# Forgetting attention and a SwiGLU block in one kernel: batch 0's queries and keys loaded and turned by two heads instead of four, and the gates of its first query tiles by one-hot matmuls

## The chip, the cores and the metric

One core of a Trainium2 chip runs the whole kernel. The metric is the device time of a run in microseconds. Its five engines have a queue each: PE (matmuls), DVE (vector), ACT (scalar functions), POOL (GpSimd: masks, casts and the issue of some DMAs) and SP (issue of the other DMAs).

## The reference

Batch 8, 8 heads, 576 positions, head size 64; then 4608 tokens of 512 features through a feed-forward block of 1536.

```python
def _attn_ref(q, k, v, f):
    scores = scale * np.matmul(q, k.transpose(0, 1, 3, 2))
    log_f = np.log(np.clip(f, 0.0001, 1.0))
    cum = np.cumsum(log_f, axis=-1)
    decay = cum[:, :, :, None] - cum[:, :, None, :]
    scores = np.where(causal, -1000000000.0, scores + decay)
    attn = np.exp(scores - np.max(scores, axis=-1, keepdims=True))
    attn = attn / (np.sum(attn, axis=-1, keepdims=True) + 1e-09)
    return np.matmul(attn, v)

def _moe_ref(x, w_gate, w_val, w_out):
    g = x @ w_gate
    return (g / (1.0 + np.exp(-g)) * (x @ w_val)) @ w_out
```

The attention output, with heads side by side, is `x` of the second function.

## The kernel before

The work is recorded as operations, each with an engine, a cost, what it comes after, buffers that it takes, and a key. `Plan.run` goes through time with these costs, and gives each engine the ready operation with the lowest key whose buffers are free. So the order on every engine is fixed when the kernel is built, by costs, keys and `ready` times; on the chip each engine works its queue in that order and waits on semaphores. PSUM has eight banks in four pools: `f` (4), `s` (2), `o` (1), `t` (1).

Attention of one head has scores in transposed form (keys on partitions, queries along the free axis), cut into the four `BANKS` so that nothing above the causal diagonal's blocks is computed. Bank 0 holds the first 256 queries (two tiles of 128). For each bank: scores on PE, `expo` on ACT (with the scale), `mask` on POOL for the diagonal blocks, `weigh` on PE against V with a column of ones, which gives the sum for the division. `invert` and `scale` on DVE divide, `flip` on PE turns the result, `put` copies it into `xT`, which the feed-forward part (`gate`, `tanh`, `silu`, `times`, `project`) reads.

The decay is added inside the score matmuls. For batches 1 to 7 four more rows of queries and keys carry it (a high, middle and low part of the key's cumulated logarithm, and the query's), brought through DRAM by `dec_out` and `rows`.

Batch 0 can't wait for that. Its gates are laid out in `KG` and `QG`, 128 partitions each, four groups of 32 rows: `KG` has the high part of the keys in rows 0 to 31 (`hi` for `hi0`), ones in rows 32 to 63, middle and low parts in rows 64 to 127 (`mid`, `low`); `QG` has ones, and the query's cumulated value in rows 32 to 63 (`up`). `choose` multiplies `QG` by a column of `chosen`, which is one in the four rows of one head and zero elsewhere: `G0[h]` for the first 256 queries and `G1[h]` for the rest. A matmul of `KG` with such a tile adds the decay of that head. The chain that makes them is recorded in `gates`: loads of `f`, `clip` (DVE), `ln` (ACT), `scan` (DVE), then `up` and `hi0` (ACT), `hi`, `rest1`, `mid`, `low` (DVE), for the first 256 columns and then for the other 320. The same for batch 1 to 7 (`lf1`) is begun in the same place.

Batch 0's queries and keys come in by `ld_quad`, each with 128 partitions: two neighbouring heads (64 partitions each) and, along the free axis, the two heads four further. `turn` transposes them on PE in two steps of 5 and 4 blocks into two banks, and `straighten` copies the bank to `QK`. The pair of heads `jj` and `jj + 4` is then scored together by `score2` on the two halves of the array, followed by the gate matmuls. While the kernel starts, and nothing is ready, `dummy` gives PE a matmul of the identity on 256 columns.

The constants (`blank`) are filled by DVE at the start: the ones in `KG` and `QG` ("lay"), in V's columns, in `PT` ("pt") and in `ones`. `warm` loads ACT's tables. `PACE0` sets from which planned time on the loads of batch 2 and later may go.

Of the kernel before, what the change touches and what calls it, by code (L numbers as in the profile page):

```python
# [33 lines left out]
class Plan:  # L34
# [150 lines left out]

HALF = 256
BANKS = [
    [(0, 0, 256), (1, 128, 128)],
# [11 lines left out]
PACE_A = 8.8  # L200
PACE0 = 64.0
LEAD = 14.0
# [3 lines left out]
def kernel(ctx, tc, q, k, v, f, w_gate, w_val, w_out, out):  # L206
# [44 lines left out]
    OT = [sb(f"ot{i}", [P, DM], F32) for i in range(NOT)]  # L251
    ident = sb("ident", [P, P], BF16)
    chosen = sb("chosen", [P, H], F32)
    warm = sb("warm", [1, 1], F32)
# [12 lines left out]
    REST = S - HALF  # L267
    G0 = [xT[:, 3, 2 * S + HALF * n : 2 * S + HALF * (n + 1)] for n in range(4)]
    G0 += [xT[:, r, S + HALF * n : S + HALF * (n + 1)] for r in (2, 3) for n in range(2)]
    G1 = [xT[:, n // 3, 2 * S + REST * (n % 3) : 2 * S + REST * (n % 3 + 1)] for n in range(H)]  # L270
# [51 lines left out]
    def clip(e, lf, c):  # L322
        nc.vector.tensor_scalar(out=lf[:, c], in0=lf[:, c], scalar1=1e-4, scalar2=1.0, op0=ALU.max, op1=ALU.min)

# [45 lines left out]

    def choose(e, h, part):
        c = slice(0, HALF) if part == 0 else slice(HALF, S)
        nc.vector.tensor_scalar_mul((G1 if part else G0)[h], QG[:, c], chosen[:, h : h + 1])  # L373

    def gates(parts, key):
# [3 lines left out]
        done, s = [], None  # L379
        a = op(("DVE", 0.45), clip, lf, slice(0, S), after=lds, key=key)  # L380
        lns = [op(("ACT", 0.15 + (c.stop - c.start) / 1100), ln, lf, c, after=[a], key=key + 0.1 * i, tag="ln")
               for i, c in enumerate(parts)]
        for i, c in enumerate(parts):
            kk = key + 11 * i
            w = c.stop - c.start
            s = op(("DVE", 0.1 + w * 0.0024), scan, cum, lf, c, after=[lns[i], s], key=kk, tag="scan")
            u = op(("ACT", 0.15 + w / 1100), up, c, after=[s, o_lay], key=kk + 0.1, tag="up")
            h = op(("DVE", 0.05 + w * 0.0011), hi, slice(64, P), c, after=[s], key=kk, tag="hi")
            h0 = op({"ACT": 0.15 + w / 1100, "DVE": 0.05 + w * 0.0011}, hi, slice(0, GR), c, after=[s, o_lay], key=kk + 0.2, tag="hi0")
            r = op(("DVE", 0.05 + w * 0.0015), rest1, c, after=[h], key=kk)  # L390
            m = op(("DVE", 0.05 + w * 0.0011), mid, c, after=[r], key=kk)
            l = op(("DVE", 0.05 + w * 0.0013), low, c, after=[m], key=kk, tag="low")
            done.append([u, h0, l])
        every = [x for d in done for x in d]
        outs = [op(("SP", SPi), dec_out, 0, n, after=every, key=-7, dma=0.15, packet=50, tag="decout") for n in range(4)]
        a = op(("DVE", 0.45), clip, lf1, slice(0, S), after=[ld1], key=key + 0.3)
        a = op(("ACT", 0.67), ln, lf1, slice(0, S), after=[a], key=key + 0.3, tag="ln1")
# [11 lines left out]
    def blank(e, what):  # L409
        if what == "qk":  # L410
            nc.vector.memset(QK[:, :, 1, 2 * S :], 0.0)
        elif what == "pt":
            for t in PT:
                for c in PADS:
                    nc.vector.memset(t[:, c : c + D], 1.0)  # L415
        elif what == "edge":
            nc.sync.dma_start(out=qk_dram[:, HSD:], in_=QK[: 2 * B, 0, 1, 2 * S :])
        elif what == "ones":
            nc.vector.memset(ones, 1.0)
        elif what == "ones_q":  # L420
            nc.sync.dma_start(out=dec_dram[0, 1], in_=ones)
        elif what == "ones_k":
            nc.sync.dma_start(out=dec_dram[1:, 0].rearrange("r h s -> h r s"),
                              in_=ones.unsqueeze(1).to_broadcast([BH, 3, S]))
        elif what == "lay":
            nc.vector.memset(QG, 1.0)
            nc.vector.memset(KG[GR : 2 * GR], 1.0)
        elif what == "chosen":
            nc.vector.tensor_add(chosen, ident[:, :H], ident[:, GR : GR + H])
            for r in (64, 96):  # L430
                nc.vector.tensor_add(chosen, chosen, ident[:, r : r + H])
        else:
            nc.vector.memset(VB[what][:, :, :, D:], 1.0)
            nc.vector.memset(VB[what][LAST:, NB - 1], 0.0)
# [3 lines left out]
              after=[op(("DVE", 0.07), lambda e: nc.vector.memset(warm, 1.0), key=-30)])  # L438
    o_lay = op(("DVE", 0.5), blank, "lay", key=-29)
    dec0, out0, out1 = gates(SPLIT, -25)  # L440
    o_warm = op(("ACT", 1.4), lambda e: nc.scalar.activation(warm, cum[:1, :1], AF.Exp), after=[dec0[0][0]], key=-19.5)
    o_id = op(("POOL", 0.6), lambda e: make_identity(nc, ident[:, :]), key=-18)
    o_vb = [op(("DVE", 0.45), blank, i, key=-7 if i < FIRST else 40 + 2000 * i, ready=0 if i < FIRST else 15) for i in range(NVB)]
    o_chosen = op(("DVE", 0.4), blank, "chosen", after=[o_id], key=-26)
    picked = [[op(("DVE", 0.33), choose, h, part, after=[o_chosen] + [d[0] for d in dec0[: part + 1]] + (dec0[0] + dec0[1] if part else []),
                  key=PICK_KEY[part][h % 4], tag=("pick", part, h)) for h in range(H)]
              for part in range(2)]
    o_qkz = op(("DVE", 0.5), blank, "qk", key=-6)
    o_pt = op(("DVE", 1.2), blank, "pt", key=-5)
    o_ones = op(("DVE", 0.3), blank, "ones", key=-6)  # L450
    o_edge = op(("SP", SPi), blank, "edge", after=[o_qkz], key=900, dma=0.2, ready=22)
# [18 lines left out]

    PH = [[(0, 5, 0), (5, 4, 0)], [(t, n, u) for u in range(2) for t, n in ((0, 5), (5, 4))]]

    def turn(e, b, g, x, n, bt):
        t0, nt, u0 = PH[b][n]
        t = ps(bt).bitcast(BF16)
        for i in range(nt):
            for u in range(2) if b == 0 else [u0]:
                r = slice(D * (u - u0), D * (u - u0 + 1))
                nc.tensor.transpose(t[r, i * P : (i + 1) * P], QN[b][2 * g + x][:, u, (t0 + i) * D : (t0 + i + 1) * D], ident)  # L479

    def straighten(e, b, g, x, n, bt):
        t0, nt, u = PH[b][n]
        slot, r = (hq2[b][g].i, slice(0, P)) if b == 0 else (hqk[b * FB + 2 * u + g].i, slice(0, D))
        dst = QK[r, slot, x, : 2 * S].rearrange("p (j c t) -> p j c t", j=2, t=QT)[:, :, :, t0 : t0 + nt]
# [60 lines left out]
    turns, rows1 = [], []  # L545

    def quad(b, g, key, ready=0.0):
        done = [[], []]
        for x in range(2):
            kk = key + x  # L550
            o1 = op(("POOL", SW), ld_quad, b, g, x, key=kk, dma=1.8, packet=107, ready=ready, tag=("quad", b, g, x))
            for n, (t0, nt, u) in enumerate(PH[b]):
                bt = Buf("t", ("f", TURN_F))
                o2 = op(("PE", (1.5 if b == 0 else 1.0) * mm(*[P] * nt)), turn, b, g, x, n, bt, after=[o1, o_id], take=[bt],
                        key=kk, tag=("turn", b, g, x))
                turns.append(o2)
                done[u].append(op(
                    {"ACT": act(nt * P), "DVE": dve(nt * P)}, straighten, b, g, x, n, bt, after=[o2, o_qkz],
                    use=[bt, hq2[b][g] if b == 0 else hqk[b * FB + 2 * u + g]], key=kk, tag=("str", b, g, x)))
        if b == 0:  # L560
            for j in range(2):
                q_ready[0, 2 * g + j] = done[0]
        else:
            for u in range(2):
                p = b * FB + 2 * u + g
                r = op(("SP", SPi), rows, p, after=[o_qkz] + out0 + o_out1, use=[hqk[p]], key=key, dma=0.25, ready=ready,
                       tag=("rows", p))
                rows1.append(r)
                for j in range(2):
                    q_ready[2 * p + j] = done[u] + [r]  # L570

# [30 lines left out]
    def score2(e, b, jj, i, bs):  # L602
# [13 lines left out]
        for n, (kt, q0, w, c) in enumerate(segs):  # L616
            for u in range(2):
                s, h, end = ps(bs[u]), jj + 4 * u, n == len(segs) - 1
                m = min(P, S - kt * P)
                g, q1 = (G0[h], q0) if i == 0 else (G1[h], q0 - HALF)  # L620
                nc.tensor.matmul(s[:m, c : c + w], KG[:, kt * P : kt * P + m], g[:, q1 : q1 + w], start=False, stop=end)  # L621

# [93 lines left out]
    def attention2(b, key, parts):  # L716

        bx = {}
        for n, (bks, qb, nq) in enumerate(parts):
            ahead = len(parts) > 1 and n == 0  # L720
            got = {}
            for jj in range(4):
# [4 lines left out]
                for m, i in enumerate(bks):  # L727
                    bs = [Buf("s", ("f", F_UNTIL)) for _ in range(2)]
                    segs = [x[2] for x in BANKS[i]]
                    cost = mm(*segs) * 3 + 0.2  # L730
                    gate_rows = dec0[i > 0] + dec0[0] + [picked[i > 0][h % H] for h in heads]
                    a = op(("PE", cost), score2, b, jj, i, bs, after=q_ready[b, jj] + gate_rows, take=bs,
# [126 lines left out]

    quad(0, 0, -20)  # L860
    quad(0, 1, -15)
    for n in range(NB):
# [35 lines left out]
V1_KEY = 400  # L898
PICK_KEY = ((-19.5, -18.5, -14.5, -14.4), (0.5, 100.5, 200.5, 300.5))
V1_AT = 16.0  # L900
# [43 lines left out]
```

## Time and profile before

| | |
|---|---|
| runs, us | 389.14, 389.13, 389.35 (median 389.14) |
| profiled execution, us | 389.19 |
| its span, us | 387.5 |
| PE busy | 377.8 us, 98% of the span, 3097 matmuls |
| DVE, ACT, POOL busy | 221.0, 214.4, 140.1 us |
| PE's clock granted | 1.0 |
| landing of batch 0's loads (queries, keys, queries, keys) | 6.35, 7.81, 9.93, 11.86 us |

Times within the execution are counted in microseconds from the start of the span; `L479` is line 479 of the kernel. In rows of groups the figures after the bar are busy us and mean ns of one, then idle time ahead of them. In the timeline they are start and duration, in brackets the idle time ahead and what ended it. Matmuls are pipelined: those in a row start sooner after each other than one lasts.

### The profile page before, as it was taken

The page shows a single profiled execution, that of the slowest core. Times are in us where ns is not written, and L with a number is a line of the kernel's source. Part 1 is how long each engine was busy: PE and PEld are TensorE (multiplying, and loading weights), DVE is VectorE, ACT ScalarE, POOL GpSimd, SP SyncE. Part 2 cuts the span into 40 slices and gives each one's busy share as a digit, 9 for nine tenths or more (in the row PEclk, how much of TensorE's full clock was granted, in tenths as well). Part 3 has the DMA queues.
Part 4 walks back from the last instruction along what each step waited for, and adds up shares of the span by engine and source line. Part 5 has one row for each costly group of instructions (what it writes and reads, how often), then busy time and mean ns, then how long its engine had stood idle before and what let it go on. Part 6 is the DMA issues. An engine that isn't in the chain of part 4 may idle for free.

```text
span 387.5 us, 8340 instructions
## 1 busy us (share of the span) xinstructions
PE 377.8 (98%) x3097; PEld 216.3 (56%) x3097; DVE 221.0 (57%) x466; ACT 214.4 (55%) x442; POOL 140.1 (36%) x368
## 2 busy tenths in 40 slices
PE   5999999999999999999999999999999999999995
PEld 3667889456556555555555555555554444444442
DVE  8958978247723774176525872376427725733750
ACT  4989974266656465755667457557673323323321
POOL 8796647036433452444355236513330000000000
PEclk9999999999999999999999999999999999999999
DMA  8999997689477998999699949994231011002002
GB/s 152 198 189 193 210 201 121 136 188 193 96 142 179 190 156 116 214 230 184 124 190 234 180 94 217 194 184 82 65 89 44 0 57 54 1 29 81 2 17 91
DMA packets 122760, 51.50 MB, mean 133 GB/s; under 512 B 109792, under 2 KB 116960, under 8 KB 121952
## 3 DMA queue, kind: packets, MB, share of 16 engines
q1 hardware_dynamic: 106336, 35.68, 45.7%
q0 software_dynamic: 16288, 15.14, 26.8%
q8 instruction: 24, 0.39, 0.4%
q14 instruction: 16, 0.13, 0.1%
q10 hardware_dynamic: 96, 0.15, 0.1%
HBM read 38.63 MB, written 17.11 MB: 144 GB/s over the span
## 4 chain that ended last, share of the span: by engine, by line
PE 94%; DVE 4%; ACT 1%; issue 0%; DVEq 0%; ACTq 0%
PE ps L793 48%; PE ps L808 24%; PE ps L596 10%; PE ps L648 7%; PE ps L479 1%; PE ps L621 1%; DVE xT L373 1%; PE ps L665 1%; PE ps L614 1%; DVE QK L304 1%; DVE PT L415 0%; DVE xT L330 0%; ACT xT L326 0%; ACT QK L302 0%; ACT QK L326 0%
## 5 line engine op out<-in xcount | busy, mean ns | idle before, releaser
L801 DVE SCALAR_TENSOR_TENSOR th<-th,ps 128x512 f32<-128x512 f32 (+1 forms) x120 | 75.6, 630 | 70.6 <-ACT th L797 70.4
L797 ACT ACTIVATE th<-ps 128x512 f32<-128x512 f32 (+1 forms) x120 | 66.5, 554 | 87.1 <-PE ps L793 85.0
L793 PE MATMUL ps<-xT,wv 128*128 128x512 bf16 (+1 forms) x480 | 113.0, 357 | 0.0
L793 PE MATMUL ps<-xT,wg 128*128 128x512 bf16 (+1 forms) x480 | 112.9, 357 | 0.0
L625 ACT ACTIVATE PT<-ps 128x320 bf16<-128x320 f32 (+2 forms) x192 | 92.2, 507 | 24.9 <-PE ps L596 17.0
L808 PE MATMUL ps<-wo,hh 128*128 128x512 bf16 x432 | 104.4, 379 | 0.0
L804 DVE TENSOR_TENSOR hh<-th,ps 128x512 bf16<-128x512 f32 (+1 forms) x120 | 76.1, 634 | 12.9 <-PE ps L793 1.2
L634 POOL TENSOR_SCALAR_AFFINE_SELECT PT<-PT 128x128 bf16<-128x128 bf16 (+1 forms) x192 | 52.6, 279 | 74.2 <-ACT PT L625 69.0
L793 PEld LDWEIGHTS <-wg 128*128 128x128 bf16 x480 | 45.2, 97 | 39.1
L793 PEld LDWEIGHTS <-wv 128*128 128x128 bf16 x480 | 45.5, 97 | 36.7
L596 PE MATMUL ps<-QK 68*128 68x256 bf16 x392 | 64.2, 261 | 0.0
L808 PEld LDWEIGHTS <-hh 128*128 128x128 bf16 x432 | 40.9, 97 | 38.8
L634 POOL TENSOR_SCALAR_AFFINE_SELECT PTa<-PTa 128x256 bf16<-128x256 bf16 x64 | 25.9, 408 | 74.3 <-ACT PTa L625 72.7
L655 DVE RECIPROCAL rc<-ps 128x5 f32<-128x5 f32 (+2 forms) x68 | 12.9, 190 | 62.1 <-PE ps L648 61.9
L648 PEld LDWEIGHTS <-PT 128*128 128x128 bf16 x768 | 36.8, 97 | 13.6
L648 PE MATMUL ps<-VB,PT 128*128 128x65 bf16 x768 | 43.7, 193 | 0.0
L812 ACT ACTIVATE ot<-ps 128x512 f32<-128x512 f32 x36 | 21.5, 598 | 38.3 <-PE ps L808 36.8
L625 ACT ACTIVATE PTa<-ps 128x384 bf16<-128x384 f32 x64 | 30.5, 487 | 13.8 <-PE ps L596 13.5
L596 PEld LDWEIGHTS <-QK 68*128 68x128 bf16 x392 | 30.8, 97 | 12.1
L660 DVE TENSOR_TENSOR xn<-ps,rc 128x320 bf16<-128x320 f32 (+2 forms) x72 | 32.2, 453 | 2.1
L648 PEld LDWEIGHTS <-PTa 128*128 128x128 bf16 x192 | 13.8, 98 | 10.9
L304 POOL CAST VB<-natv 128x512 bf16<-128x512 f32 (+1 forms) x32 | 19.2, 622 | 0.0
(62 smaller groups left out, 167.6 us busy)
## 6 DMA issues: line engine op xcount, KB each, us to landing
out_dram<-ot SPq DMA_DIRECT2D x36, 256.0 KB
natv<-in_v_dram SPq DMA_DIRECT2D x25, 256.0 KB
qk_d<-in_q_dram POOLq DMA_DIRECT2D x24, 144.0 KB, 3.2
qk_d<-in_k_dram POOLq DMA_DIRECT2D x24, 144.0 KB, 4.4
wg<-in_moe_w_gate_dram POOLq DMA_DIRECT2D x3, 512.0 KB, 11.1
wv<-in_moe_w_val_dram POOLq DMA_DIRECT2D x3, 512.0 KB, 12.9
wo<-in_moe_w_out_dram POOLq DMA_DIRECT2D x4, 384.0 KB, 14.4
xT<-in_q_dram POOLq DMA_DIRECT2D x4, 288.0 KB, 9.0
```

The costliest lines, as they stand in the source:

```text
L304: E[e].tensor_copy(dst, src)
L596: nc.tensor.matmul(s[:, c : c + w], QK[:KR, hqk[p].i, 1, j * S + kt * P : j * S + (kt + 1) * P], QK[:KR, hqk[p].i, 0, j * S + q0 : j * S + ...
L625: nc.scalar.activation(place(h, i)[:, OFFS[i] : OFFS[i] + c], ps(bs)[:, :c], AF.Exp, scale=0.125)
L634: nc.gpsimd.affine_select(out=d, in_=d, pattern=pat, compare_op=ALU.is_ge, fill=0.0, base=0, channel_multiplier=-1,)
L648: nc.tensor.matmul(o[:, lo : lo + D + 1], pt[:, c : c + P], VB[hvb[b].i][:, kt, hb, : D + 1], start=first and n == 0, stop=last and n == l ...
L660: nc.vector.tensor_mul(XN[bx.i][:, qb : qb + nq, j], o, r)
L793: nc.tensor.matmul(ps(bf)[:, :n], w[:, ko, fc * P : (fc + 1) * P], xT[:, ko, t0 : t0 + n], start=(ko == 0), stop=(ko == KD - 1))
L797: nc.scalar.activation(TH[bt.i][:, :n], ps(bf)[:, :n], AF.Tanh, scale=0.5)
L801: nc.vector.scalar_tensor_tensor(out=t, in0=t, scalar=1.0, in1=ps(bf)[:, :n], op0=ALU.add, op1=ALU.mult)
L804: nc.vector.tensor_mul(HH[bh.i][:, lo : lo + n], TH[bt.i][:, :n], ps(bf)[:, :n])
L808: nc.tensor.matmul(ps(bf)[:m, :DM], HH[hs[fc].i][:, lo : lo + m], wo[:, fc, :], start=(fc == 0), stop=(fc == KF - 1))
L812: nc.scalar.activation(OT[bo.i][:m], ps(bf)[:m, :DM], AF.Copy, scale=0.5)
```

## The change

Batch 0's queries and keys are loaded by `ld_two`: one pair of heads (`jj` and `jj + 4`) with 64 partitions at a time, eight loads where there were four, in the order queries, keys of pair 0, of pair 1, and so on. `turn_two` transposes the nine blocks of both heads (18 matmuls of 64 columns) into one bank, and `straighten_two` copies the 576 columns of it. So a pair depends on its own loads alone.

For bank 0 `choose` and `G0` go. The gate of a head is added by two matmuls: `KG` against a one-hot column of `three` (the identity's rows of the three key parts, repeated along the queries), and the identity's column of the head's `up` row, repeated along the keys, against `QG`.

The fills of ones write pairs of bf16 as one f32 (`ONE2`), with half the elements. The clip of batch 0 is split in two, 256 and 320 columns; that of batch 1 to 7 goes to POOL. Some keys are others: the second part of the gates (`PART1`), the remaining picks, `PACE0` 62 instead of 64.

In the order of the built kernel: POOL issues four of the loads ahead of the identity and four after it, then V's first load, batch 1's clip, the rest of V, the weights; PE has 11 fillers ahead of the first turn instead of 17 and 13 in all instead of 37; ACT does the first straightening ahead of `up` and `hi0`.

```diff
+ONE2 = 1.0019378662109375
-PACE0 = 64.0
+PACE0 = 62.0
...
+    three = sb("three", [P, H], BF16)
...
     def clip(e, lf, c):
-        nc.vector.tensor_scalar(out=lf[:, c], in0=lf[:, c], scalar1=1e-4, scalar2=1.0, op0=ALU.max, op1=ALU.min)
+        E[e].tensor_scalar(out=lf[:, c], in0=lf[:, c], scalar1=1e-4, scalar2=1.0, op0=ALU.max, op1=ALU.min)
...
-    def choose(e, h, part):
-        c = slice(0, HALF) if part == 0 else slice(HALF, S)
-        nc.vector.tensor_scalar_mul((G1 if part else G0)[h], QG[:, c], chosen[:, h : h + 1])
+    def choose(e, h):
+        nc.vector.tensor_scalar_mul(G1[h], QG[:, HALF:], chosen[:, h : h + 1])
...
-        a = op(("DVE", 0.45), clip, lf, slice(0, S), after=lds, key=key)
...
         for i, c in enumerate(parts):
-            kk = key + 11 * i
+            w = c.stop - c.start
+            a = op(("DVE", 0.1 + w / 960), clip, lf, c, after=lds, key=key - 1 + 0.1 * i, tag="clip")
+            lns.append(op(("ACT", 0.15 + w / 1100), ln, lf, c, after=[a], key=key + 0.1 * i, tag="ln"))
+        for i, c in enumerate(parts):
+            kk = key if i == 0 else PART1
...
-        a = op(("DVE", 0.45), clip, lf1, slice(0, S), after=[ld1], key=key + 0.3)
+        a = op(CLIP1, clip, lf1, slice(0, S), after=[ld1], key=key + 0.3, tag="clip1")
...
-                    nc.vector.memset(t[:, c : c + D], 1.0)
+                    E[e].memset(t[:, c : c + D].bitcast(F32), ONE2)
...
-            nc.vector.memset(ones, 1.0)
+            E[e].memset(ones.bitcast(F32), ONE2)
...
-            nc.vector.memset(QG, 1.0)
-            nc.vector.memset(KG[GR : 2 * GR], 1.0)
+            nc.vector.memset(QG.bitcast(F32), ONE2)
+            nc.vector.memset(KG[GR : 2 * GR].bitcast(F32), ONE2)
         elif what == "chosen":
-            nc.vector.tensor_add(chosen, ident[:, :H], ident[:, GR : GR + H])
-            for r in (64, 96):
-                nc.vector.tensor_add(chosen, chosen, ident[:, r : r + H])
+            nc.vector.tensor_add(three, ident[:, :H], ident[:, 64 : 64 + H])
+            nc.vector.tensor_add(three, three, ident[:, 96 : 96 + H])
+            nc.vector.tensor_add(chosen, three, ident[:, GR : GR + H])
         else:
-            nc.vector.memset(VB[what][:, :, :, D:], 1.0)
+            nc.vector.memset(VB[what][:, :, :, D:].bitcast(F32), ONE2)
...
+    def ld_two(e, jj, x):
+        a = srcs["qk"[x]][:H].rearrange("(u j) (p t) d -> j p u (t d)", u=2, p=QP)
+        g, j = divmod(jj, 2)
+        nc.gpsimd.dma_start(out=QN[0][2 * g + x][QP * j : QP * (j + 1)], in_=a[jj])
+
+    def turn_two(e, jj, x, bt):
+        g, j = divmod(jj, 2)
+        r, t = slice(QP * j, QP * (j + 1)), ps(bt).bitcast(BF16)
+        for i in range(QT):
+            for u in range(2):
+                nc.tensor.transpose(t[D * u : D * (u + 1), i * QP : (i + 1) * QP],
+                                    QN[0][2 * g + x][r, u, i * D : (i + 1) * D], ident[r, r])
+
+    def straighten_two(e, jj, x, bt):
+        g, j = divmod(jj, 2)
+        dst = QK[:, hq2[0][g].i, x, j * S : (j + 1) * S].rearrange("p (c t) -> p c t", t=QT)
+        copy(e, dst, ps(bt).bitcast(BF16)[:, :S].rearrange("p (t c) -> p c t", t=QT))
...
-                g, q1 = (G0[h], q0) if i == 0 else (G1[h], q0 - HALF)
-                nc.tensor.matmul(s[:m, c : c + w], KG[:, kt * P : kt * P + m], g[:, q1 : q1 + w], start=False, stop=end)
+                keys = KG[:, kt * P : kt * P + m]
+                if i:
+                    nc.tensor.matmul(s[:m, c : c + w], keys, G1[h][:, q0 - HALF : q0 - HALF + w], start=False, stop=end)
+                else:
+                    nc.tensor.matmul(s[:m, c : c + w], keys, three[:, h : h + 1].to_broadcast([P, w]), start=False, stop=False)
+                    nc.tensor.matmul(s[:m, c : c + w], ident[:, GR + h : GR + h + 1].to_broadcast([P, m]),
+                                     QG[:, q0 : q0 + w], start=False, stop=end)
...
-    quad(0, 0, -20)
-    quad(0, 1, -15)
+    for jj in range(H // 2):
+        two(jj, -20 + jj)
...
-PICK_KEY = ((-19.5, -18.5, -14.5, -14.4), (0.5, 100.5, 200.5, 300.5))
+PICK_KEY = (-10, -9, 200.5, 300.5)
+PART1 = -18.5
+CLIP1 = ('POOL', 0.6)
+PT_ENG = ('DVE', 0.8)
```

`quad`, `turn` and `straighten` serve batch 1 alone now.

## The prediction

> **What bounds the kernel now.** I read the page's busy table first, then what PE waited for, PE's timeline of the first 21 us, the chain of waits over that stretch, the busy times of two stretches, and the rows of POOL.
>
> ```profile
> PE 377.8 (98%) x3097; PEld 216.3 (56%) x3097; DVE 221.0 (57%) x466; ACT 214.4 (55%) x442; POOL 140.1 (36%) x368
> ```
> ```profile
> PE ps L891 <- POOL ident masks.py:199: 3.6, 1, 3.6
> PE ps L479 <- ACT QK L302: 1.3, 1, 1.3
> PE ps L614 <- ACT QK L302: 0.4, 1, 0.4
> PE ps L614 <- DVE natv L516: 0.2, 1, 0.2
> ```
>
> PE is the bound, and all its listed waits lie before 16 us. So only two things can move the time: how early PE gets into its dense work, and how much work it has after that.
>
> ```profile
> 3.56 3.42 PE L891 MATMUL ps<-ident 128*128 128x256 bf16 x17 [3.56 <-POOL ident masks.py:199]
> 6.91 0.69 PE L479 MATMUL ps<-ident,xT 128*64 128x128 bf16 x18
> ...
> 12.16 0.34 PE L614 MATMUL ps<-QK 64*128 64x256 bf16 x4 [0.38 <-ACT QK L302]
> ...
> 15.45 0.34 PE L614 MATMUL ps<-QK 64*128 64x256 bf16 x4 [0.22 <-DVE natv L516]
> ...
> 18.92 0.27 PE L891 MATMUL ps<-ident 128*128 128x256 bf16 x1
> ```
>
> L891 is filler. L614 opens a score step of two heads: at 12.16 for heads 0 and 4, at 15.45 for heads 2 and 6, which I call the third pair. From 15.45 on PE is dense; what is left of non-work is two fillers with their gaps (18.92 to 19.33 and 19.54 to 19.65, together 0.52), a filler at 22.39 and a gap of 0.3 at 34.8.
>
> ```profile
> 7.22 0.64 ACT QK L326
> ...
> 8.73 0.65 ACT QK L302
> 9.38 0.04 issue
> 9.43 0.71 PE ps L479 x18
> 10.13 0.45 DVE xT L373 x2
> 10.58 0.74 DVE QK L304
> ```
>
> The chain of waits (start, us, what): the turned keys wait for ACT's straightening copy, which stood behind three logarithms and two gate copies; then for DVE, busy with the eight early picks (L373).
>
> **The change, part by part.** Times are on the profiled execution: span 387.5 and 389.19 with what lies around it, against a median of 389.14. Differences carry over one to one.
>
> *Fills (DVE).* Three fills of 576 elements cost 0.54 each; the rows nearest to their 288 elements are 128x256 and 64x264 uint32 at 0.27 and 0.28, so 0.30: 0.72 saved. Fifteen PT fills 0.074 apart go to about 0.04: 0.5. With VB, 1.3 in all. But DVE next needs the identity, and behind that wait stand the clip and the whole chain of the gates.
>
> *Identity (POOL).* Four half loads are now issued ahead of it, where two whole ones were. A whole load has 256 pieces and takes 0.72, a V load 0.90, a narrow one with 16 pieces 0.50:
>
> ```profile
> L491 POOL DMA_DIRECT2D qk_d<-in_q_dram x24 | 12.4, 517 | 0.0
> L509 POOL DMA_DIRECT2D VB<-in_v_dram x8 | 7.1, 903 | 0.0
> L468 POOL DMA_DIRECT2D xT<-in_k_dram x4 | 2.9, 722 | 0.0
> ```
>
> A half load has 128 pieces and lies between 0.50 and 0.72; I take 0.65, nearer to its own line. From 1.32: 0.80 + 3 x 0.65 = 4.07, and 0.6 for the identity: ready at 4.7 (bounds 4.1 and 5.0) instead of 3.5. The chosen columns end at 5.2 instead of 5.93.
>
> *Gates.* The clip of the first 256 columns takes about 0.29 for 0.46; the logarithm starts at 5.55 instead of 6.44. The scan no longer stands behind batch 1's clip (0.2 lost there): 6.0 instead of 7.06. Scan to low took 2.23, so DVE has the first gates at 8.2 instead of 9.3.
>
> *First turn.* 11 fillers at 0.213 run from 4.72 to 7.07. Without them the first loads would be the next thing late: the whole ones landed at 6.35 and 7.81, the halves carry half the bytes. A turn now has 18 matmuls of 64 columns; before, 18 of 128 took 0.5. Its cost lies between 0.26 (columns count) and 0.5 (instructions count): 0.4. ACT can straighten the first queries at 7.75 (bounds 7.2 and 8.3).
>
> *ACT's chain from there,* by starts: copy 0.62, two gate copies 0.78, batch 1's logarithm 0.68, table 1.40 (it stood 9.99 to 11.40), copy 0.62, two gate copies 0.85, copy 0.60: first exponential at 13.3, about the old 13.19. That is the catch: the first scores can start at 9.2 instead of 12.16, but their evacuation hardly moves. What moves is what follows: before, after one exponential ACT went back to gates and a copy until 15.16; now the exponentials come nearly in a row, with one copy between them.
>
> *The third pair.* The second pair needs ACT's second copy, done at 11.95: 12.0 to 13.05. Two turns, 0.8 and a change of tile 0.1, end at 13.95; the first exponential has freed the bank at 13.75. Third pair at 14.05 (bounds 13.4 and 14.7): 1.4 earlier.
>
> *Added on PE.* Bank 0 of a pair streams 768 more columns, at 0.109 per 256: 0.33. The first two pairs lie ahead of the dense part, so 0.65 counts; a stride-0 operand has no row, and at twice the price would add 0.33. Three weighing matmuls at 0.03 that stood ahead of 15.45 come later: 0.09. Sum +0.74.
>
> *Taken off.* The order of the changed kernel has one filler in the dense part and not three, and more score steps ready there: 0.5 off; the gap at 34.8 I leave.
>
> *Hidden.* The early picks leave DVE (8 instructions, 1.9 us), which was not the bound after 16. The gate rows and the load bytes are the same. PACE0 moves later loads by 2 us of plan: hidden under PE, and nothing if not used. Batch 1's first loads and the weights are queued behind the same bytes (weights landed at 19.5 and 22.2, first used at 33.2); without that slack a late landing would cost PE its delay. POOL gets 2.2 of issues and batch 1's clip (0.6 to 1.6 by the cast's 0.62 and DVE's 0.81) ahead of the V loads, weights, a query load and the masks, less 2.2 of waits that it had: its first mask goes from 13.72 to 14.6. ACT's logarithm of batch 1, which has the table load and the second copy queued behind it, waits for that clip from 9.2 on; the clip is done at 9.0. The weighing matmuls wait for the masks: I allow 0.2.
>
> Sum: -1.4 + 0.74 - 0.5 + 0.2 = -1.0, so **388.2**.
>
> **The rivals.** *ACT takes it back.* These two rows bracket the dense start:
>
> ```profile
> 15.44:20.56 5.12, 4.97 (x63) 3.27 (x63) 5.02 (x18) 4.35 (x12) 4.99 (x11) 1.00 1.24 216
> 20.56:34.80 14.24, 14.24 (x216) 10.33 (x214) 9.23 (x27) 12.78 (x27) 10.48 (x29) 1.00 1.58 185
> ```
>
> The columns are PE, its weight loads, DVE, ACT, POOL. ACT is at 90% in the second. The changed order puts all of batch 0's exponentials and more of batch 1's copies ahead of the first feed-forward matmul: 16 exponentials of 0.37, 8 of 0.49, 8 of 0.31 and 15 others, some 22 us from 13.3, so 35.3 at best, where PE arrives at 35.7. If the queue's hiccups cost PE 0.7 to 1.1, the time is 388.9 to 389.3. Against: PE then also waits less on batch 1.
>
> *The clock (slower).* The fillers before show it:
>
> ```profile
> 3.56 2.96 PE L891 MATMUL ps<-ident 128*128 128x256 bf16 x13 [3.56 <-POOL ident masks.py:199]
> ```
>
> Those up to 6.3 start 0.213 apart, those after it 0.109: the rate doubled 2.85 after the first. Now 11 fillers last 2.35, and then come turns with gaps. If PE stays at half rate through the start, a turn costs 0.8, a score step 2.1, and the first scores start at 9.65: 9.65 + 2.1 + 1.7 (two turns) puts the second pair at 13.5, and 2.0 and 1.7 more put the third at 17.3. That is 1.85 + 0.74 - 0.5 = +2.1: **391.3**. It turns slower once the rate doubles later than some 12.5. For it: less unbroken filler; against: the matmuls go on without a long gap. The Trainium skill (TensorE: Matmul & The Clock Gate, Part 1) has the clock released after a busy window of about 3.4 us that runs freely, and its Part 4 says that transposes do not count as busy in the same way. By that rule the turns would not help, and this rival's 391.3 would be the time; the trace, with 2.85, agrees in part only.
>
> *Masks late on POOL.* With 0.72 an issue and 1.6 for the clip, the first masks come at 16 and hold up weighing by 1 to 1.5, and the logarithm delays ACT by 0.8: 389.9.
>
> *The loads aren't what was late,* so halving does nothing: then only fills and gates count. In my sum that is nearly so already, since ACT's chain sets the second pair; it is the forecast's low end of gain, 388.6, and its chance is in the forecast's.
>
> **How the numbers follow.** Gain carried over, about 388.2: 0.43, and with the cheap ends (issue 0.50, turn 0.26) 387.0: 0.10. ACT takes it back, about 389.1: 0.25. Masks, 389.9: 0.12. Clock, 391.3 at worst: 0.10. Two tenths of a per cent, 0.8 us, is about what a measurement of this kernel can tell from no change, so faster is below 388.4: 0.53; same 0.25; slower 0.22. The forecast's own range is 387.2 to 388.6; the whole range, from the cheap ends to the masks, 387.0 to 389.9, leaves out most of the clock.
>
> **What would show it.** Identity ready near 4.7; low at 8.2; ACT's first copy near 7.75 and first exponential near 13.3; the third pair (now a score step of heads 2 and 6) near 14.05; 0.33 more per bank-0 step. A third pair later than 15.2, matmuls still 0.2 apart per 256 columns after 9, or PE idle behind POOL's masks or ACT between 15 and 36 would make it wrong.

## The result, and the profile after

| | before | after |
|---|---|---|
| median, us | 389.16 | 391.09 |
| lowest to highest, us | 388.90 to 391.18 (13 executions) | 389.41 to 391.71 (13) |
| ratio to before | | 1.0037, 95% interval 1.0021 to 1.0053 |
| profiled execution, us (span) | 389.19 (387.5) | 389.41 (387.6) |
| first exponential (ACT), first mask (POOL) | 13.19, 13.72 | 14.09, 15.65 |
| third pair's score step | 15.45 | 15.26 |

The change makes the kernel slower, by 0.4% (the medians alone give 0.5%); 388.2 was forecast. The profiled execution of after happens to be its fastest. A second one, taken later under the label "again", took 390.95, near the median, and is shown beside it.

The page's busy table and what PE waited for, after:

```profile
PE 378.7 (98%) x3161; PEld 217.4 (56%) x3161; DVE 221.2 (57%) x461; ACT 213.0 (55%) x439; POOL 144.3 (37%) x373
```
```profile
PE ps L918 <- POOL ident masks.py:199: 4.5, 1, 4.5
PE ps L481 <- DMA xT<-in_q_dram: 0.4, 1, 0.4
```

By these two views PE does better than before: the waits for ACT and DVE (1.3, 0.4, 0.2) are gone. What is wrong shows only in PE's timeline, in how long the same form of instruction takes:

```profile
4.49 2.53 PE L918 MATMUL ps<-ident 128*128 128x256 bf16 x11 [4.49 <-POOL ident masks.py:199]
6.95 1.17 PE L481 MATMUL ps<-ident,xT 64*64 64x64 bf16 x36
8.52 0.69 PE L481 MATMUL ps<-ident,xT 64*64 64x64 bf16 x18 [0.40 <-DMA xT<-in_q_dram]
...
10.09 0.50 PE L636 MATMUL ps<-QK 64*128 64x256 bf16 x4
...
13.01 0.50 PE L636 MATMUL ps<-QK 64*128 64x256 bf16 x4
...
14.57 0.76 PE L481 MATMUL ps<-ident,xT 64*64 64x64 bf16 x36
15.26 0.34 PE L636 MATMUL ps<-QK 64*128 64x256 bf16 x4
```

Columns are start, duration, engine, line, operation, tile, shape. Four score matmuls of 64x256 take 0.50 at 10.09 and 13.01, and 0.34 at 15.26; before they took 0.34 from the first on (12.16). 36 turning matmuls take 1.17 at first and 0.76 later. PE runs at half rate until 14.2, where 256 columns go from 0.213 apart to 0.109; before, that happened between 6.3 and 6.5. In the execution taken again it goes on longer:

```profile
15.66 0.50 PE L636 MATMUL ps<-QK 64*128 64x256 bf16 x4
...
17.49 0.61 PE L636 MATMUL ps<-QK 64*128 64x192 bf16 x4
18.02 0.82 PE L644 MATMUL ps<-xT 128*128 128x192 bf16 x4
18.68 0.35 PE L675 MATMUL ps<-VB,PTa 128*128 128x65 bf16 x6
18.96 0.34 PE L636 MATMUL ps<-QK 64*128 64x256 bf16 x4
```

There the third pair (15.66) is still at half rate and the rate doubles near 18.5. The granted clock in the table by stretches stays at 1.00 for these stretches, in both executions; it does not show this half rate, the rows do. The trace holds no record of the granted clock before the doubling: its first one, with full rate, is at 14.23 in the one execution and at 18.49 in the other.

The second finding is on POOL and ACT:

```profile
7.76 2.14 POOL L323 TENSOR_SCALAR QK<-QK 32x576 f32<-32x576 f32 x1
```
```profile
9.94 0.68 ACT L326 ACTIVATE QK<-QK 32x576 f32<-32x576 f32 x1 [0.74 <-POOL QK L323]
10.64 1.28 ACT L442 ACT_TABLE_LOAD   x1
...
14.09 1.21 ACT L652 ACTIVATE PTa<-ps 128x384 bf16<-128x384 f32 x3
```

Batch 1's clip took 2.14 on POOL, and ACT's logarithm waited 0.74 for it, with the table load and the second copy queued behind.

### The profile page after: what moved, and what is told of

The parts are those of the page before. It is cut to its first block, busy times and chain, and to the rows that moved or that the text cites. A ratio compares the mean times of both kernels' runs of the same rounds, so it can differ in the third digit from the quotient of the medians.

```text
span 387.6 us, 8453 instructions
## 1 busy us (share of the span) xinstructions
PE 378.7 (98%) x3161; PEld 217.4 (56%) x3161; DVE 221.2 (57%) x461; ACT 213.0 (55%) x439; POOL 144.3 (37%) x373
## 4 chain that ended last, share of the span: by engine, by line
PE 97%; DMA 1%; ACT 0%; POOL 0%; issue 0%; ACTq 0%; POOLq 0%
PE ps L820 48%; PE ps L835 24%; PE ps L618 10%; PE ps L675 8%; PE ps L644 2%; DMA xT<-in_q_dram 1%; PE ps L636 1%; PE ps L496 1%; PE ps L692 1%; PE ps L481 1%; PE ps L646 1%; PE ps L647 0%; POOL xT L474 0%; ACT QK L302 0%; ACT ot L839 0%
## 5 line engine op out<-in xcount | busy, mean ns | idle before, releaser
L652 ACT ACTIVATE PT<-ps 128x512 bf16<-128x512 f32 (+2 forms) x192 | 92.6, 507 | 25.9 <-PE ps L618 20.0
## 6 DMA issues: line engine op xcount, KB each, us to landing
wv<-in_moe_w_val_dram POOLq DMA_DIRECT2D x3, 512.0 KB, 13.3
```

The lines of the kernel that those rows point to most:

```text
L652: nc.scalar.activation(place(h, i)[:, OFFS[i] : OFFS[i] + c], ps(bs)[:, :c], AF.Exp, scale=0.125)
```

## The experiments

Theory CLOCK: too little filler, and turns that load PE too lightly, keep PE at half rate until 14 to 19. Rival POOL: the clip delays ACT, the V loads and the masks, and that is the loss. Rival ADDED: one-hot matmuls and half loads cost more than they bring. All results first; "doubles" is where the profiled execution goes to full rate, by its first record of the granted clock. The kernel before was run beside each, with medians of 388.95 to 389.17; ratios are against those. The profiled execution of a kernel need not be a typical one.

| kernel | median, us (n) | lowest, highest | ratio to before | doubles |
|---|---|---|---|---|
| changed, again | 390.95 (1) | | | 18.5 |
| early filler | 391.34 (5) | 390.24, 391.55 | 1.0055 (1.0043 to 1.0067) | 4.5; half again 14.8 to 18.2 |
| clip on DVE | 390.50 (12) | 388.20, 392.01 | 1.0032 (1.0010 to 1.0054) | 17.2 |
| both | 388.45 (12) | 388.13, 390.35 | 0.9989 (0.9976 to 1.0001) | 6.9 |
| early filler, waits filled, clip on POOL | 389.27 (11) | 389.21, 389.76 | 1.0006 (0.9997 to 1.0015) | 4.7 |
| both, waits filled | 388.39 (12) | 388.12, 389.48 | 0.9979 (0.9967 to 0.9990) | 4.4 |
| the same less 8 one-hot matmuls | 388.31 (12) | 387.64, 389.82 | 0.9974 (0.9959 to 0.9989) | 4.0 |
| before with 11 fillers | 389.65 (11) | 388.91, 390.86 | 1.0013 (0.9999 to 1.0026) | 13.2 |
| before, 128x128 transposes | 389.17 (10) | 388.92, 389.76 | 0.9996 (0.9985 to 1.0007) | 9.0 |
| before, 64x64 transposes | 393.65 (4) | 393.43, 393.81 | 1.0117 (1.0103 to 1.0131) | 17.4 |
| before, half array | 389.68 (12) | 389.23, 391.27 | 1.0010 (0.9999 to 1.0022) | 12.8 |
| before, full array, short | 389.55 (11) | 388.89, 391.94 | 1.0007 (0.9992 to 1.0022) | 7.0 |
| clip on DVE, full turns | 393.13 (9) | 392.17, 394.92 | 1.0088 (1.0059 to 1.0118) | 7.4; half again 14.2 to 21.0 |
| clip on DVE, first turns full | 390.31 (12) | 388.49, 391.70 | 1.0013 (0.9991 to 1.0034) | 20.1 |

### The changed kernel again

> The changed kernel itself, for the profile of another execution. CLOCK: if its time is near 391.5, the rate doubles near 17.5 instead of 14.2 and the third pair starts near 17; if near 390.2, the rate doubles earlier and falls back once. POOL and ADDED: the doubling has nothing to do with the time.

Its profile is shown above: 390.95, doubling near 18.5 and not 17.5, the third pair at 15.66 and not 17. Of these two executions the one whose rate doubles later takes longer, as CLOCK has it.

### Early filler, clip on DVE, both

```diff
# early filler (in dummy): the first 32 fillers read a constant tile
+ for _ in range(1 if seen else 22):
+     if len(seen) < 32:
+         nc.tensor.matmul(z[:, :HALF], QG[:, :P], QG[:, :HALF], start=True, stop=True)
...
+     seen.append(i)
# clip on DVE, in the same place of the program
- E[e].tensor_scalar(out=lf[:, c], in0=lf[:, c], scalar1=1e-4, scalar2=1.0, ...)
+ nc.vector.tensor_scalar(out=lf[:, c], in0=lf[:, c], scalar1=1e-4, scalar2=1.0, ...)
```

> The changed kernel with 32 fillers ahead of the first turn instead of 11; they read a constant tile that DVE fills first, so that they start near 1.5 us instead of 4.49. The order of every other engine is the same. Theory CLOCK (too little filler ahead of the turns leaves PE at half rate until 14.2): the rate doubles some 3 us after the first filler, by 5; turns take 0.5 and not 1.0; first scores near 9.3 (10.09), second pair near 12.1, set by ACT's second copy (13.01), third pair near 14.6 (15.26), held by the first exponential, which still comes at 14.1; the time is 388.5 to 389.3, at or below the kernel before. Rival POOL (the clip of 2.14 us on POOL delays ACT, the V loads and the masks): no more than 0.3 off, 390.5 or more. Rival ADDED (one-hot matmuls and half loads cost more than they bring): 390.5 or more.

> The changed kernel with batch 1's clip issued on DVE at the same place of the program; PE and ACT keep their order, POOL loses one instruction, DVE gains one behind its first scan. POOL: the clip takes under 0.5 instead of 2.14, ACT's logarithm starts near 9.2 (9.94), first exponential near 13.4 (14.09), first mask near 14.0 (15.65); 389.3 or less. CLOCK: the same moves on ACT and POOL, but the matmuls stay 0.21 apart until 13 or later, the third pair stays within 0.4 of 15.26 and the time within 0.5 of the changed kernel's 391.1. ADDED: as CLOCK, for another reason.

> The changed kernel with both edits: 32 early fillers and batch 1's clip on DVE. CLOCK and POOL both: doubling by 5, first exponential near 13.4, third pair near 14.0, 388.0 to 388.7, what the prediction gave. CLOCK alone: as with the early fillers alone, 388.5 to 389.3. POOL alone: as with the clip alone. ADDED: 389.6 or more in spite of the full rate, because the 0.65 of one-hot matmuls and the fourth pair of loads remain.

The early filler alone did what CLOCK expected to the rate (4.5) and nothing for the time: 391.34, where CLOCK had 388.5 to 389.3. PE's timeline of that kernel says why. The execution shown, 390.24, is the fastest of its five; the other four took 391.34 to 391.55, at a mean granted clock of 0.989 to 0.991 against 0.993.

```profile
10.59 0.76 PE L481 MATMUL ps<-ident,xT 64*64 64x64 bf16 x36
12.71 0.34 PE L636 MATMUL ps<-QK 64*128 64x256 bf16 x4 [1.37 <-ACT QK L302]
...
14.63 0.43 PE L636 MATMUL ps<-QK 64*128 64x256 bf16 x4
...
16.92 1.03 PE L644 MATMUL ps<-xT 128*128 128x192 bf16 x4
...
18.22 0.34 PE L636 MATMUL ps<-QK 64*128 64x256 bf16 x4
```

PE, now fast, waits 1.37 for ACT's second copy, the one that stands behind the clip on POOL. Some two us later its rate falls back to half and stays there from about 14.8 to 18.2, while PE is dense. This fall the table by stretches does show, in its column of the granted clock (the one after POOL's):

```profile
8.00:11.50 3.50, 2.92 (x85) 2.19 (x85) 3.37 (x6) 2.02 (x4) 3.44 (x3) 1.00 1.37 198
11.50:14.90 3.40, 2.18 (x52) 1.59 (x52) 3.27 (x6) 3.34 (x9) 3.40 (x5) 0.98 1.86 122
14.90:18.20 3.30, 3.30 (x26) 2.01 (x22) 2.50 (x9) 2.63 (x7) 3.30 (x7) 0.51 1.33 149
```

The clip on DVE took 0.60 there, the first exponential came at 13.20 and the first mask at 13.88, as POOL expected; the time, 390.50, is nearer to CLOCK's (within 0.5 of 391.1) than to POOL's 389.3. Its executions lie between 388.20 and 392.01, and the profiled one (390.60) doubles at 17.2. Three of the twelve took 388.20 to 388.57, as little as with both edits; they were not traced. By the medians neither edit does it alone. Both together give 388.45:

```profile
9.95 0.34 PE L636 MATMUL ps<-QK 64*128 64x256 bf16 x4 [0.37 <-DVE QK L304]
...
12.32 0.34 PE L636 MATMUL ps<-QK 64*128 64x256 bf16 x4 [0.58 <-ACT QK L302]
...
14.38 0.34 PE L636 MATMUL ps<-QK 64*128 64x256 bf16 x4
```

All three score steps are at full rate, and the third pair is at 14.38. So ADDED falls, since its matmuls and loads are all still there, and the two causes are not a sum: with the clip on POOL a fast PE waits, and loses its rate by waiting.

### The waits filled

```diff
# in score2, ahead of bank 0 of the first and the second pair
+ for _ in range({0: 3, 1: 4}.get(jj, 0) if b == 0 and i == 0 else 0):
+     nc.tensor.matmul(ps(bs[0])[:, :HALF], ident, ident.unsqueeze(1).to_broadcast([P, 2, P]), start=True, stop=True)
# with the clip on POOL: {0: 3, 1: 11}; 32 early fillers there, 30 with the clip on DVE
```

> The changed kernel with 32 early fillers, batch 1's clip left on POOL, and fillers in PE's waits (three ahead of the first score step, eleven ahead of the second, where 1.56 was idle). CLOCK: the rate no longer falls back near 15; 388.7 to 389.4 where the same kernel without these 14 fillers had 391.34; what is left against the kernel with both edits (388.45) is the clip's own delay on ACT, 0.4 to 0.7. Rival (the clip's delay itself costs the 2.9 between those two): 390.5 or more.

> The changed kernel with batch 1's clip on DVE, 30 early fillers, and seven fillers more in PE's two remaining waits (three ahead of the first score step, four ahead of the second). CLOCK: no window with long idle time is left, so the rate does not fall back once it has doubled; most executions at 388.1 to 388.5, fewer stragglers than the kernel with both edits (which had 390.35, 389.41 and 389.05 among 12); ratio to before 0.997 to 0.9995. Rival (the remaining scatter is not PE's rate, or the fillers push the scores back): as that kernel or up to 0.5 worse.

With the early fillers in and the clip still on POOL, fillers in the waits bring 391.34 to 389.27, and all 11 executions within 0.55. The wait of 1.37 is now filler, and the third pair stays at full rate:

```profile
11.75 1.38 PE L634 MATMUL ps<-ident 128*128 128x256 bf16 x11
...
14.78 0.34 PE L638 MATMUL ps<-QK 64*128 64x256 bf16 x4
```

PE did no useful work in that time before or after; only its rate was kept. What is left to 388.39, about 0.9 (0.4 to 0.7 was expected), goes with the clip. In the profiled executions (389.24, and 388.45 with both edits) 0.40 of it lies ahead of the third pair (14.78 and 14.38) and 0.39 behind it, where no wait of PE is listed; the cause of this second part stays open.

The kernel with both edits and filled waits beats the kernel before (388.39, ratio 0.9979) and the changed one; its lowest, 388.12, is where the forecast lay. Against the kernel with both edits alone (388.45) it gains nothing clear: three of twelve executions are at 389.0 or more in each. Its profiled execution, 389.07, is one of them and is at full rate from 4.4 on; PE waited 1.44 and 0.82 there for loads of queries and keys. So not all of the scatter is PE's rate.

### The added matmuls

```diff
# both, waits filled; bank 0 of the third and fourth pair
+ if jj > 1:
+     continue
  nc.tensor.matmul(s[:m, c : c + w], ident[:, GR + h : GR + h + 1].to_broadcast([P, m]), ...)
```

> As the kernel with gap fillers, but in bank 0 of the third and fourth pair the second of the two one-hot matmuls (the keys' half of the gates, L647 there) is left out: 8 matmuls, 1536 columns, so the scores of those heads lack a term. ADDED, as the prediction has it: 0.65 of PE work on the path, 387.5 to 387.9 where the kernel with gap fillers has 388.1 to 388.5. Rival (the exponentials on ACT hold this stretch, so the added matmuls are hidden): within 0.2 of the kernel with gap fillers.

The scores of those heads lack a term in this kernel; it is for timing alone. The median moved by 0.08, the lowest execution by 0.48. By the median that is the rival's answer (hidden), and 0.65 was not reached by either. The profiled execution (389.66) is a slow one, in which PE waits for DVE where it did not (0.56, 0.38 and 0.87 between 14 and 20). How much of the 0.65 is on the path the scatter does not tell.

### What holds the rate down: the kernel before with other fillers

Here the rest of the program is that of before, in the same order.

```diff
# 11 fillers: the 12th to 17th are left out
# 128x128 transposes, two for each filler
+ nc.tensor.transpose(z.bitcast(BF16)[:, n * P : (n + 1) * P], ident, ident)
# 64x64 transposes, eight for each
+ nc.tensor.transpose(z.bitcast(BF16)[D * u : D * (u + 1), n * D : (n + 1) * D], ident[:D, :D], ident[:D, :D])
# half array, four for each of the first 17
+ nc.tensor.transpose(z.bitcast(BF16)[:, n * D : (n + 1) * D], ident[:D, :], ident[:D, :D])
# full array, short, four for each of the first 17
+ nc.tensor.matmul(z[:, n * D : (n + 1) * D], ident, ident[:, :D], start=True, stop=True)
```

> The kernel before with six of its 17 first fillers left out, so that 11 stand ahead of the first turn as in the changed kernel; every other engine keeps its order. CLOCK: the burst ends near 5.9, the rate doubles later than 9 in some or all executions; with a doubling near 14 the first scores move from 12.16 to about 12.6 and the third pair from 15.45 to about 17, 390.5 to 391; with an earlier one less. POOL and ADDED: 389.1, no change.

> The kernel before with each filler made of two transposes of 128 columns instead of one matmul of 256; every other engine keeps its order. If transposes count for PE's rate as matmuls do: doubling near 6.4, 388.9 to 389.3. If they do not: half rate past the first scores, doubling at 13 or later, 389.6 to 391.3, at least as slow as the kernel before with 11 fillers (389.65).

> The kernel before with each filler made of eight transposes of 64x64 (two side by side on the same 64 rows, four times), the form that the changed kernel's turns have, where the transposes of 128x128 were tried already; the columns streamed per filler are about the same, every other engine keeps its order. CLOCK, refined (such tiles use half of the array and count for less): the rate is still half at the first scores, doubling after 13, as with 11 fillers or later; 389.6 to 391. If they count as full tiles do: doubling by 9 in the profile, 388.9 to 389.3, as with the 128x128 transposes (389.17).

> The kernel before with each of its 17 first fillers made of four transposes on 64 rows and 128 columns of the array, 64 columns streamed each: the duration of a filler is the same, half of the array is used, and PE has 51 instructions more and not 170 as with the 64x64 transposes, so that it does not run into the stop at its 223rd matmul. If half an array counts for less: rate still half at 9 and at the first scores, 389.6 or more. If only PE's time counts: doubling by 9, 388.9 to 389.3.

> The control for the half array: the kernel before with each of its 17 first fillers made of four matmuls of 64 columns on all 128 rows and 128 columns, the same number of instructions and the same streaming time. By both theories of the array's share: doubling by 7 to 9, 388.9 to 389.3. If short instructions as such keep the rate down: as the half array, 389.6 or more.

Six fillers fewer move the doubling from 6.5 to 13.2 and the median by 0.5 (0.7 against the 388.95 of the kernel before run beside it); the interval of the ratio still includes 1, and CLOCK's 390.5 to 391 was not reached. The third pair moved from 15.45 to 16.16, not to 17: a late doubling costs the kernel before less, in part because it uses up waits that PE had there (the 0.4 and 0.2 are no longer listed). The 128x128 transposes cost nothing: the rate doubled at 9.0, after transposes alone. The two kernels that differ in nothing but the share of the array, first the half array, then the full one:

```profile
3.56 3.80 PE L896 MATMUL ps<-ident 64*128 64x64 bf16 x68 [3.56 <-POOL ident masks.py:199]
7.29 1.17 PE L479 MATMUL ps<-ident,xT 128*64 128x128 bf16 x18
8.40 1.03 PE L898 MATMUL ps<-ident 128*128 128x256 bf16 x4
...
12.96 0.34 PE L614 MATMUL ps<-QK 64*128 64x256 bf16 x4
```
```profile
3.57 3.71 PE L896 MATMUL ps<-ident 128*128 128x64 bf16 x68 [3.57 <-POOL ident masks.py:199]
7.21 0.69 PE L479 MATMUL ps<-ident,xT 128*64 128x128 bf16 x18
7.84 0.61 PE L898 MATMUL ps<-ident 128*128 128x256 bf16 x4
```

Both fill PE from 3.56 to 7.2. After the full array the first turn takes 0.69, after the half array 1.17, and PE, busy almost without a break from 3.56 on, doubles only at 12.8. These are two traces. By the time the kernels are not told apart (medians 389.68 and 389.55, and 388.9 to 389.3 was expected of the full array), but no execution of the half array came under 389.23. In the kernel with 64x64 transposes, 7.7 us of unbroken work (3.56 to 11.3) did not release the rate. Its 393.65 is more than the rate costs: PE also stood still for 1.17 from 11.3 on, waiting for nothing that the profile shows.

The turns of the changed kernel are of this kind: two 64x64 transposes side by side on the same 64 rows, half the array, where before they used all 128 rows.

### Full turns in the changed kernel

```diff
# clip on DVE; in turn_two, on the other 64 rows, into a bank not in use
+ o, z = slice(QP * (1 - j), QP * (2 - j)), bank[2 if j else 6].bitcast(BF16)
+ for u in range(2 if jj < 3 else 0):      # first turns full: jj < 1
+     nc.tensor.transpose(z[D * u : D * (u + 1), i * QP : (i + 1) * QP], ident[o, o], ident[o, o])
```

> The changed kernel with batch 1's clip on DVE and no filler more than the changed kernel has (11 ahead of the first turn), but each 64x64 transpose of the first three turned pairs accompanied by one on the other 64 rows, into a bank that is not read then: 108 transposes more, so that a turn fills all four quarters of the array. CLOCK, refined (the rate is released by how much of the array is busy, and quarter tiles count for less): the rate doubles by 11 and not at 14 to 18.7, and in spite of the added work the time falls from 390.5 (the clip on DVE alone) to 389.2 or less. Rival (it is not the tiles' size, only the missing filler or PE's gaps): doubling as late as before, 390.5 or more, up to 391.5 where the added transposes take time of their own.

> As the kernel with full turns, but only the first two turned tiles (heads 0 and 4) get the accompanying transposes: 36 transposes more instead of 108, so that PE reaches its 223rd matmul, where two kernels stood still for 1.2 and 2.8 us waiting for nothing that the profile shows, only near 16 and not near 11. CLOCK, refined: the rate doubles near 7.3 as it did there, with 11 fillers ahead as in the changed kernel; no stall; 388.3 to 389.3, where the clip on DVE alone has 390.5. Rival (the stall comes with any added transposes, or the early doubling does not carry over to the time): 390.5 or more.

With full turns the rate doubled at 7.4 behind the same 11 fillers, as expected; but the first turn had begun only at 6.91, so most of the work ahead of the doubling was the fillers. The time was worse, 393.13, which neither side expected. What PE waited for (L485 is the accompanying transpose):

```profile
PE ps L921 <- POOL ident masks.py:199: 4.5, 1, 4.5
PE ps L485 <- issue: 2.8, 1, 2.8
```

A stop of 2.84 from 11.6 to 14.45 with nothing to wait for, and with it the fall back to half rate, from 14.2 until 21.0. This stop and the one of 1.17 with the 64x64 transposes come behind the same instruction: 223 matmuls and 226 weight loads had started in both. It could be PE's instruction supply; the Trainium skill (Runtime: NRT & Kernel Launch, Instruction fetch mechanics) has engines refill their instructions in blocks, by DMA, mostly hidden. The traces fit that: every one has a first transfer of 16 KB of kind "instruction" within the kernel's first 17 us, here from 12.18 to 13.15, within the stop, and with the 64x64 transposes from 10.01 to 10.89, just ahead of the stop. PE had started 223 and 198 matmuls when they began; in the other 14 traces, which have no such stop, 110 to 168. That PE waited for this transfer is not recorded, so the stop's cause was not shown.

With only the first two turns full, there is no stop, but the profiled execution (391.70, the slowest) doubled at 20.1, and the median, 390.31, is that of the clip on DVE alone (390.50). So full tiles in the first turns are not enough.

**What the traces say together.** The two attempts seem to point to opposite sides; the records of the granted clock go some way to explain it. The first stretch at full rate lasts 6.83 with full turns, 10.24 with the early filler, and 368.64, 372.05, 375.47, 378.88 or 382.29 in the other traces: all are whole multiples of 3.41. So the rate changes only at the ends of windows of 3.41, and these can be counted back from the first record. In each window one can add up the time in which PE streams columns (0.213 for 256 of them at half rate), with each matmul weighted by the part of the array that it uses, rows times columns over 128 x 128. The table gives both sums as shares of the window; where matmuls overlap, the weighted one can come out 0.01 higher.

| kernel, window | PE streams | weighted | then |
|---|---|---|---|
| before, 3.04 to 6.45 | 0.85 | 0.85 | full |
| before, 64x64 transposes, 3.74 to 7.15 | 1.00 | 0.50 | half |
| before, half array, 5.99 to 9.41 | 0.87 | 0.70 | half |
| before, 128x128 transposes, 5.55 to 8.96 | 0.92 | 0.93 | full |
| changed, 3.99 to 7.40 | 0.81 | 0.75 | half |
| changed, again, 8.25 to 11.67 | 0.81 | 0.67 | half |
| the same, 11.67 to 15.08 | 0.87 | 0.68 | half |
| the same, 15.08 to 18.49 | 0.84 | 0.81 | full |
| full turns, 3.96 to 7.37 | 0.81 | 0.81 | full |
| first turns full, 3.03 to 6.44 | 0.58 | 0.59 | half |
| the same, 6.44 to 9.86 | 0.72 | 0.58 | half |

The 16 traces have 41 windows that PE went through at half rate with a weighted share above 0.05. All 16 with a weighted share of 0.79 or more ended at full rate, all 21 with 0.74 or less stayed at half, and four at 0.75 and 0.76 went two each way. Without the weight there is no such bound: from 0.78 to 1.00 both occur. By this reckoning the changed kernel's turns do hold the rate down: it and the kernel with full turns have a window at nearly the same place (3.99 and 3.96), with the 11 fillers and the first turn in it and 0.81 streamed, and the turn's weight makes the difference between 0.75 and 0.81. Where the windows fall decides the rest: with first turns full they split the fillers, and neither half was enough.

**What stays open.** The bound of about 0.75 was found in the same traces that it sorts, some matmul records can be missing from them, and no kernel was built to test it. What places the windows in an execution is not shown.

## Why the prediction was wrong

**The failed step is the clock.** The sum took PE at full rate from the first turn on (a turn at 0.4, the second pair's step from 12.0 to 13.05) and so put the third pair at 14.05; it stood at 15.26 and 15.66, and in the second execution 2.83 us more at half rate followed. The prediction had this as a rival at 0.10, "391.3 at worst", with the mechanism and the total nearly right: +0.21 for the third pair, 1.42 lost at half rate behind it, and the sum's own +0.74 and -0.5 make +1.9; measured is 390.95 - 389.19 = +1.8. Its parts were not right, so the total is partly luck: it had a half-rate turn at 0.8 and the whole loss ahead of the third pair, at 17.3; two turns took 1.10, and most of the loss came behind it.

What was wrong above all is its weight. The one argument against it, "the matmuls go on without a long gap", is true and didn't help: PE went on from 4.5 to 18.5 at half rate. "It turns slower once the rate doubles later than some 12.5" is what all three traces with the changed kernel's fillers and turns show (14.2, 17.2, 18.5). The rule of the Trainium skill (TensorE: Matmul & The Clock Gate, Part 4) that I set beside it, that transposes do not count as busy in the same way, pointed the right way for a wrong reason here: 128x128 transposes alone released the rate at 9.0; those on half of the array did not. By the window that ended at 9.0, 128x128 transposes counted as matmuls do (0.93).

**The clip on POOL** was bounded at 0.6 to 1.6 and took 2.14. POOL reached it at 7.76, the clip was done at 9.90 instead of 9.0, ACT's second copy began at 12.04 and the first exponential at 14.09 instead of 13.3 (13.20 with the clip on DVE). The first mask came at 15.65, not 14.6. The masks' rival named this, with 389.9.

**The loads.** A half load took 0.62 to issue (0.65 forecast). But the halves landed one after the other: 5.33, 6.09, 8.48 and 9.22. The same four heads that two whole loads brought by 7.81 are there at 9.22. The built order turns the second pair ahead of the first scores, so these came at 10.09, not 9.2; at full rate, in the kernel with both edits, still at 9.95.

**What held.** Identity 4.44 (4.7 forecast), chosen 5.04 (5.2), logarithm 5.38 (5.55), scan 5.83 (6.0); low ended half a us late, at 8.71 (8.2). At full rate the last transposes of a turn start 0.28 after its first, at the cheap end of 0.26 to 0.5. ACT did not take the gain back: the views list no wait of PE for ACT in the changed kernel. With rate and clip repaired, the kernel with both edits has the third pair at 14.38 (14.05 forecast): -1.07, +0.74, -0.5 gives -0.83, and its profiled execution took 388.45, -0.74. The same reckoning, with half of the time that PE runs at half rate behind the third pair added, gives 390.3 for the early filler (390.24 measured), 390.5 for the clip on DVE (390.60), 393.4 for full turns (393.23), 392.0 for first turns full (391.70) and 389.2 for the first execution of the changed kernel (389.41); only with the waits filled and the clip on POOL is it 0.5 off (388.8 for 389.24). So the sum from the third pair on was sound as a whole, though no run confirms its 0.65 by itself; what set the third pair was not.

## What to carry to other kernels

When a change shortens or splits what PE does in its first microseconds, ask first whether PE still gets to its full rate, and read that from the duration of one form of matmul early and late, not from busy shares or waits. Count work that fills half of the array as half, and keep PE fed through the waits of the start: fillers there cost nothing that these runs show, and 14 of them were worth 2 us here. Of two causes that each do nothing when repaired alone, try both together before dropping either.

## What the runs showed of the hardware

- PE's rate doubled 2.7 to 5.6 us after the first of an unbroken row of full-array matmuls (early fillers: from 1.32 to 4.0, 4.4, 4.5, 4.7 and 6.9; before: 3.56 to 6.5). The same kernel doubled at 14.2 in one execution (389.41) and at 18.5 in another (390.95).
- The rate changed at the ends of windows of 3.41, and went to full where PE streamed for at least some 0.75 of one, each matmul counted by its share of the array (41 windows, four of them at the bound). Transposes of 128x128 counted as matmuls do (0.93, then full).
- It fell back once PE had waited 1.37 in some 3.4 us, and came again 3.4 later. The Trainium skill (TensorE: Matmul & The Clock Gate, Part 1) has an idle window of about 3.4 ahead of a fall; here PE was busy for 2.18 of the 3.40 before it. By the weighted share the windows ahead of the two falls had 0.34 and 0.13, and the lowest that kept full rate 0.41.
- The granted clock shows the fall back (0.51) and not the half rate at the start (1.00).
- The same clip of 32x576 f32 took 2.14 on POOL and 0.60 on DVE.
